# A linear-attention and mixture-of-experts kernel: other places for the routing and for the weight parts

## The chip, the cores and the metric

The kernel runs on one core of one Trainium2 chip. The core has five engines that each work through their own queue in order: TensorE (PE, with weight loads PEld), VectorE (DVE), ScalarE (ACT), GpSimd (POOL) and SyncE (SP, which here only issues DMAs). They wait for each other by semaphores. The metric is the device time of one execution in microseconds (us); of several runs the median counts.

## The reference

```python
def _attn_ref(r, k, v, w, u):                 # B, H, S, D = 4, 8, 768, 48
    state = zeros((B, H, D, D)); y = zeros_like(r)
    for t in range(S):
        kt, vt, rt = (k[:, :, t], v[:, :, t], r[:, :, t])
        cur = einsum('bhd,bhe->bhde', u[None] * kt, vt)
        y[:, :, t] = einsum('bhd,bhde->bhe', rt, state + cur)
        state = w[None, :, :, None] * state + einsum('bhd,bhe->bhde', kt, vt)
    return y

def _moe_ref(x, w_gate, w_noise, noise, w1, w2):   # N, D, E, F = 3072, 384, 8, 1024
    noisy_logits = x @ w_gate + log1p(exp(x @ w_noise)) * noise
    top2 = argpartition(-noisy_logits, 2, axis=1)[:, :2]
    top2_w = softmax of the two logits
    for e in range(E):
        for k in range(2):
            mask = top2[:, k] == e
            h = maximum(x[mask] @ w1[e], 0.0)
            out[mask] += top2_w[mask, k, None] * (h @ w2[e])
    return out
```
`reference()` runs the attention, lays its result out as 3072 tokens of 384 numbers, and gives that to the experts. All tensors are float32.

## The kernel before

**Attention.** The recurrence is cut into chunks of 128 steps: 6 chunks of 4 batches give NT = 24 tiles, in the order chunk by chunk. The loop over tiles (L958) is written so that neighbouring tiles overlap. One pass, here called turn i, puts out, in this order on each engine's queue:

- `load(i + 3)` on SP: k, r and v of a later tile.
- `trans(i + 1)`: TensorE transposes the decayed k (`kd`) and r; ScalarE copies the first to kT, VectorE multiplies the second into rT.
- `xtrans(i - 1)` and `zup(i - 1)`: the transposed output x of the tile before, and the state update (zt on VectorE, z and zb on ScalarE).
- `uterm_b(i + 1)`: a sum c on VectorE, then cv = v * c, on VectorE up to tile 8 and from tile 9 on as eight small ScalarE instructions (L327).
- `prep_k(i + 2)` and `uterm_a(i + 2)`: the products kd (L307) and rku (L314, L316) on GpSimd, each in two halves of 4 heads.
- one or two calls of `wstep` (weights, below), then `rstep(STEPS_A)` (routing, below).
- `yout(i)` on TensorE (L388 and L396), which needs the masked scores `am` of tile i; `xout(i)`: x on VectorE, and its store.
- `logits(i - 1)`, then `rstep(STEPS_B)`.
- `scores(i + 1)` on TensorE (L346; needs kT and rT), `mask(i + 1)` on VectorE (L354, two pieces), `kvup(i)` on TensorE (L364), then `rstep(STEPS_KV)`.

**Weights.** Each expert's W1 (three parts of 128 x 1024) and W2 (four parts of 128 x 768) is split into a high and a low part, so that products are nearly exact. A part is a generator in `w_split`: a DMA on SP into one of three staging buffers, then three empty places, then the copy of the high part on ScalarE (L279), then the subtraction of the low part on VectorE (L281). `wstep` moves each part in work on by one place and starts a new one if fewer than three are in work. Each call is one place.

**Routing.** The tiles fall into three groups of eight (GROUPS). When a group's logits are there, `route(g)` is queued: a generator of some 80 small VectorE instructions (noise term, the two largest logits, ranks, lists) with a few TensorE products among them. `rstep(us)` adds `us` to a credit, cuts the credit at 1.6 * us + 0.2, and then puts out routing until the credit is used up; most places of the generator cost 0.2. Where the generator says "pe", or where a group is newly queued, `at_pe` is set to `gap` = 2: the next call only counts down and returns, with its credit kept, and the one after it goes on. In turn 22 (I_EARLY) the lists of expert 0's first 512 tokens must be there, and its first tokens are gathered.

**Experts.** `seq` lists pieces (expert, chunk): expert 0 has three, the others two. A piece is `p1` (first product, eight steps of 9 products L841, then a ReLU on ScalarE L843 and a low part on VectorE L845) and `p2` (second product, L875, in groups of 128 tokens). `xT` transposes gathered tokens for the next piece. While expert 0's later pieces run, `rest(1)` and `rest(2)`, the lists of the other experts, are put out by `rest_step`; they use products with `pL` (L513) on TensorE. Expert 1's weights are queued ahead of `p2(0, 1)`, with three places at once, then two per group of tokens there and one per step of `p1(0, 2)`. From expert 1 on, one place per step carries the next expert's weights.

Of the kernel before, what the change touches and what calls it, by code (L numbers as in the profile page):

```python
# [25 lines left out]
W_MAX = 1.05  # L26
WARM0 = 8
STEPS_A = 1.2
STEPS_B = 1.1
STEPS_KV = 0.3  # L30
STEPS_P1 = 0.75
STEPS_P2 = 3.0
WARM1 = 2
# [9 lines left out]
def kernel(  # L43
# [14 lines left out]
    nc = tc.nc  # L58
    B, H, S, D = r.shape
# [198 lines left out]


    W = {}  # L260

    def w_split(e):
        W[e] = {}
        units = []

        def unit(mat, c0, c1, src):
            def f():
                if mat not in W[e]:
                    sh = [128, ND, FF] if mat == 0 else [128, NF, DM]
                    W[e][mat] = [wpool[e % 2].tile(sh, F32R, name=f"w{mat}{x}{e % 2}", bufs=1) for x in "hl"]  # L270
                hi, lo = (t[:, c0:c1, :] for t in W[e][mat])
                t = stg.tile([128, 1024], F32, name="stg")
                n = hi.shape[1] * hi.shape[2]
                tv = t[:, :n].rearrange("p (a b) -> p a b", b=hi.shape[2])
                nc.sync.dma_start(tv, src)
                yield
                yield
                yield
                nc.scalar.activation(hi, tv, AF.Copy)  # L279
                yield  # L280
                nc.vector.tensor_sub(lo, tv, hi.bitcast(F32))  # L281
                yield
            return f()

        for c in range(ND):
            units.append(unit(0, c, c + 1, w1[e, c * 128:(c + 1) * 128, :].rearrange("(c p) f -> p c f", p=128)))
        for c in range(0, NF, 2):
            units.append(unit(1, c, c + 2, w2[e, c * 128:(c + 2) * 128, :].rearrange("(c p) d -> p c d", p=128)))
        return units
# [3 lines left out]
    def wstep():  # L293
        for un in list(wrun):
            if next(un, 0) == 0:
                wrun.remove(un)
        if wq and len(wrun) < 3:
            un = wq.pop(0)
            next(un)
            wrun.append(un)  # L300
# [2 lines left out]
    AM, X, CV, PY, PA = {}, {}, {}, {}, {}  # L303

    def prep_k(i, eng=None):
        for h in (slice(0, H // 2), slice(H // 2, H)):
            (eng or nc.gpsimd).tensor_mul(kd[i % 3][:, h, :D], kt[i][:, h], tabk[:, h, :D])  # L307

    RKU = {}

    def uterm_a(i):
        rku = att.tile([128, H, D], F32, name="rku")
        for h in (slice(0, H // 2), slice(H // 2, H)):
            nc.gpsimd.tensor_mul(rku[:, h], rt[i][:, h], kt[i][:, h])  # L314
        for h in (slice(0, H // 2), slice(H // 2, H)):
            nc.gpsimd.tensor_mul(rku[:, h], rku[:, h], ub[:, h])  # L316
        RKU[i] = rku

    def uterm_b(i):
# [531 lines left out]
    def p2(e, ci, step=None):  # L851
        hb, ht = HH[e, ci]
        wh, wl = W[e][1]
        offs = {t: 128 * j for j, t in enumerate(chunks(e)[ci])}

        ts = chunks(e)[ci]
        for t in ts if (e, ci) != seq[-1] else ts[-1:] + ts[:-1]:
            n, o = tw(t), offs[t]
            py = psum.tile([128, DM], F32, name="pym", tag=f"py{np2[0] % 2}")
            np2[0] += 1  # L860
            ot = moe.tile([128, DM], F32, name="ot", bufs=NOT)
            OT[e, t] = ot
            hs = slice(o, o + n)
            if n == 64:
                for f in range(NF):
                    nc.tensor.matmul(py, ht[:, f].rearrange("p a b -> p (a b)"), wh[:, f, :], start=(f == 0), stop=(f == NF - 1),  # L866
                                     skip_group_check=True)
                    nc.tensor.matmul(py[:n], ht[:, f, 0, :], wl[:, f, :], start=False, stop=(f == NF - 1),  # L868
                                     skip_group_check=True)
                nc.scalar.activation(ot[:n], py[64:], AF.Copy)  # L870
                nc.vector.tensor_add(ot[:n], py[:n], ot[:n])
            else:
                q = [(a, x, f) for f in range(NF) for a, x in ((0, wh), (0, wl), (1, wh))]
                for j, (a, x, f) in enumerate(q):
                    nc.tensor.matmul(py, hb[:, f, a, hs], x[:, f, :], start=(j == 0), stop=(j == len(q) - 1))  # L875
                    if step and j % 8 == 7:
                        step()
                if (e, ci) == seq[-1]:
                    OT[e, t] = py
                else:  # L880
                    nc.scalar.activation(ot, py, AF.Copy)  # L881
            yield t
# [39 lines left out]

    gap, credit = [2], [0.0]

    def rstep(us):

        credit[0] = min(credit[0] + us, 1.6 * us + 0.2)
        while route_q:
            if at_pe[0] > 0:
                at_pe[0] -= 1  # L930
                if at_pe[0] > 0:
                    return
            if credit[0] <= 0:
                return
            try:
                c = next(route_q[0])
            except StopIteration:
                route_q.pop(0)
                continue
            if c == "pe":  # L940
                at_pe[0] = gap[0]
                credit[0] -= 0.3
                return
            credit[0] -= c or 0.2
# [13 lines left out]
    for i in range(NT):  # L958
        if i + NLD - 1 < NT and i + NLD - 1 > 2:
            load(i + NLD - 1)  # L960
        if i >= NT - 16:
            q = (i - NT + 16) * 192
            nc.sync.dma_start(out[q:q + 192, :].rearrange("(p two) d -> p two d", two=2),
                              zrow[:96, None, :].to_broadcast([96, 2, DM]))
        if i + 1 < NT:
            trans(i + 1)
        if i:
            xtrans(i - 1)
            zup(i - 1)
        if i == I_EARLY:  # L970
            while GEARLY - 1 not in routed:
                rstep(1)
            early()
        if i + 1 < NT:
            uterm_b(i + 1)
        if i + 2 < NT:
            prep_k(i + 2)
            uterm_a(i + 2)
        wstep()
        if i < GROUPS[0][1]:  # L980
            wstep()
        rstep(STEPS_A)
        if i == 0:
            flag = consts_c()
        if i in (0, 3):
            next(flag)
        yout(i)
        xout(i)
        if i:
            logits(i - 1)  # L990
            route_when_done(i - 1)
        rstep(STEPS_B)
        if i == NT - 1:
            for _ in xT(0, 0):
                pass
            p1a = p1(0, 0)
        if i + 1 < NT:
            scores(i + 1)
            mask(i + 1)
        kvup(i)  # L1000
        rstep(STEPS_KV)
    xtrans(NT - 1)
    next(p1a)
    logits(NT - 1)
# [28 lines left out]
    wts1 = stack.enter_context(tc.tile_pool(name="wts1", bufs=1, side="right", reuse_waits="tile"))  # L1033
    wpool[1] = wts1
    late[0] = stack.enter_context(tc.tile_pool(name="late", bufs=1, side="right", reuse_waits="tile"))
    wq.extend(w_split(1))
    for _ in range(3):
        wstep()
# [5 lines left out]
    def rest_step(us):  # L1044
        rstep(us)
        if not route_q and not listed[0]:
# [2 lines left out]
            xgather(1, 0)  # L1049
            tokens(NJ, E * NJ)  # L1050

    gap[0] = 1
    for t in p2(0, 1, lambda: rest_step(1.0)):
        if t == 3:
            for _ in xT(0, 2):
                pass
        hold.append((0, t))
        wstep()
        wstep()
    for s in range(2, len(seq)):  # L1060
        e, ci = seq[s]
        end = s + 1 == len(seq)
        if e and ci == 0:
            nxt = w_split(e + 1) if e + 1 < E else []
            wq.extend(nxt[:ND])
        elif e:
            wq.extend(nxt[ND:])
        xt = xT(*seq[s + 1]) if not end else iter(())
        for j, _ in enumerate(p1(e, ci)):
            while hold:  # L1070
                emit_out(*hold.pop(0))
            if s == 2:
                rest_step(STEPS_P1)
            elif XT_AT <= j < XT_AT + 2:
                next(xt, None)
            wstep()
        if s > 2 and s + 2 < len(seq):
            xgather(*seq[s + 2])

        for t in p2(e, ci, (lambda: rest_step(1.0)) if s == 2 else None):  # L1080
            if s > 2:
                next(xt, None)
            wstep()
            hold.append((e, t))
            while len(hold) > (0 if end else 1):
                emit_out(*hold.pop(0))
        if s == 2:
            while not listed[0]:
                rest_step(1)
            for _ in xt:  # L1090
                pass
            xgather(*seq[s + 2])
        if ci == len(chunks(e)) - 1 and not end:
            while hold:
                emit_out(*hold.pop(0))
            pgather(e + 1)
# [77 lines left out]
```

## Time and profile before

| | us |
|---|---|
| median of 3 runs (656.6 to 661.78) | 657.9 |
| the profiled execution | 665.16 |
| its span in the trace | 663.3 |
| attention, until its last scores | 170.29 |
| mean granted TensorE clock | 0.981 |

The profile shows one execution. A row of the view in order of time gives the start, the duration, the engine, the line, the operation with output and inputs, how many instructions are merged, and in brackets how long the engine had been idle before and what ended that. A row of the view by stretches gives the stretch, its length, then the busy time and the number of instructions of PE, PEld, DVE, ACT and POOL, the granted TensorE clock as a share of full speed, the DMA engines' mean busy share, and GB/s. On the page, each digit of "PEclk" is the granted clock in tenths in one of 40 equal slices. SPq is the time in which SP issues DMAs.

### The profile page before, as it was taken

Reading aid. Unit: us, or ns where it says so; the run is one execution under the profiler, and the core shown is the slowest. Engines: PE = TensorE matmul, PEld = TensorE weight load, DVE = VectorE, ACT = ScalarE, POOL = GpSimd, SP = SyncE. Lnnn points to the kernel's source line nnn. Section 1 sums busy time; section 2 is a strip of 40 time slices with the busy share of each in tenths; the row PEclk is TensorE's granted clock in tenths of the full one; section 3 lists DMA queues with packets and bytes.
Section 4 is the critical chain, followed back from the end, with each engine's and each line's share of the span. In section 5 each row is a group of like instructions: output and inputs, shape, how many; then the busy total and the mean of one; then the engine's idle time right before and its main releaser. Section 6 shows DMA issues by size and latency. Waiting matters only on the chain.

```text
span 663.3 us, 11905 instructions
## 1 busy us (share of the span) xinstructions
PE 631.3 (95%) x4436; PEld 600.9 (91%) x4437; DVE 352.1 (53%) x883; ACT 262.2 (40%) x737; POOL 260.6 (39%) x389
## 2 busy tenths in 40 slices
PE   8899899989998799999999999999999999999993
PEld 5789899988898789999999999999999999999993
DVE  7687868699479946253443625244262524523230
ACT  2455667666322424252442424234242433423220
POOL 8575534544201227422641542364164136315211
PEclk9889979999999999999999999999999999999998
DMA  7995746764304534441524334263343425302001
GB/s 127 221 238 130 168 113 169 160 152 117 109 1 128 161 126 134 132 142 70 186 82 139 117 113 136 69 186 100 121 127 108 130 78 175 103 26 85 37 2 37
DMA packets 111444, 78.87 MB, mean 119 GB/s; under 512 B 86721, under 2 KB 101441, under 8 KB 111378
## 3 DMA queue, kind: packets, MB, share of 16 engines
q1 hardware_dynamic: 101442, 49.19, 28.7%
q0 software_dynamic: 9936, 28.83, 13.9%
q8 instruction: 37, 0.61, 0.4%
q14 instruction: 29, 0.24, 0.1%
HBM read 59.03 MB, written 19.76 MB: 119 GB/s over the span
## 4 chain that ended last, share of the span: by engine, by line
PE 83%; DVE 9%; SPq 2%; issue 2%; ACT 2%; DMA 1%; POOL 0%; POOLq 0%; DVEq 0%; ACTq 0%
PE ph L841 31%; PE pym L875 30%; PE py L396 5%; PE pa L346 3%; PE ptm L820 3%; PE py L388 2%; PE pt L334 2%; PE pl L426 2%; SPq L122 2%; PE pym L868 2%; PE pym L866 2%; DVE am L354 1%; PE pwarm L364 1%; DMA stg<-in_moe_w_dram 1%; PE ptx L414 1%
## 5 line engine op out<-in xcount | busy, mean ns | idle before, releaser
L875 PE MATMUL pym<-w1h,hb 128*128 128x384 f32 x768 | 204.2, 339 | 0.0
L841 PE MATMUL ph<-xh,w0h 128*128 128x384 f32 (+3 forms) x408 | 142.6, 350 | 1.7 <-ACT xh L821 1.7
L896 POOL DMA_INDIRECT out_dram<-ot,TK x56 | 57.5, 1027 | 218.8 <-DVE ot L892 199.5
L841 PE MATMUL ph<-xl,w0h 128*128 128x384 f32 (+3 forms) x408 | 139.8, 343 | 0.5 <-DVE xl L822 0.2
L875 PEld LDWEIGHTS pym<-w1h,hb 128*128 128x128 f32 x768 | 139.6, 188 | 0.6
L841 PE MATMUL ph<-xh,w0l 128*128 128x384 f32 (+3 forms) x408 | 139.7, 342 | 0.0
L845 DVE SCALAR_TENSOR_TENSOR hb<-ph,hb 128x384 fp32r<-128x384 f32 (+1 forms) x136 | 72.5, 533 | 113.9 <-ACT ht L843 71.1
L875 PE MATMUL pym<-w1l,hb 128*128 128x384 f32 x384 | 129.5, 337 | 0.0
L843 ACT ACTIVATE hb<-ph 128x384 fp32r<-128x384 f32 (+1 forms) x136 | 64.2, 472 | 120.2 <-PE ph L841 112.7
L793 POOL DMA_INDIRECT xg<-xd,GR x56 | 53.7, 959 | 81.0 <-DVE f L675 34.2
L881 ACT ACTIVATE ot<-pym 128x384 f32<-128x384 f32 x45 | 22.1, 491 | 160.3 <-PE pym L875 160.3
L841 PEld LDWEIGHTS ph<-xh,w0h 128*128 128x128 f32 x408 | 77.3, 189 | 5.0 <-ACT xh L821 2.3
L841 PEld LDWEIGHTS ph<-xl,w0h 128*128 128x128 f32 x408 | 77.5, 190 | 3.7 <-DVE xl L822 1.2
L841 PEld LDWEIGHTS ph<-xh,w0l 128*128 128x128 f32 x408 | 77.3, 190 | 2.5
L875 PEld LDWEIGHTS pym<-w1l,hb 128*128 128x128 f32 x384 | 72.3, 188 | 0.1
L822 DVE TENSOR_TENSOR xl<-ptm,xh 128x384 fp32r<-128x384 f32 (+1 forms) x56 | 28.9, 524 | 75.1 <-ACT xh L821 53.0
L396 PE MATMUL py<-vt,am 128*128 128x96 f32 x384 | 61.3, 287 | 5.9 <-DVE am L354 5.3
L802 POOL DMA_INDIRECT pv<-out_dram,GA x49 | 55.6, 1135 | 25.9 <-issue 14.3
L396 PEld LDWEIGHTS py<-vt,am 128*128 128x128 f32 x384 | 52.9, 201 | 7.5 <-DVE am L354 7.5
L307 POOL TENSOR_TENSOR kd<-kt,tabk 128x192 f32<-128x192 f32 x46 | 27.2, 612 | 66.1 <-PE pwarm L364 58.1
L354 DVE TENSOR_TENSOR am<-pa,mneg 128x512 int32<-128x512 int32 x48 | 30.8, 682 | 12.4 <-PE pa L346 12.4
L892 DVE SCALAR_TENSOR_TENSOR ot<-ot,GT,pv 128x384 f32<-128x384 f32 (+1 forms) x46 | 27.0, 610 | 11.0 <-ACT ot L881 10.9
(206 smaller groups left out, 880.5 us busy)
## 6 DMA issues: line engine op xcount, KB each, us to landing
stg<-in_moe_w_dram SPq DMA_DIRECT2D x24, 512.0 KB, 4.1
stg<-in_moe_w_dram SPq DMA_DIRECT2D x32, 384.0 KB, 3.3
rd<-in_r_dram SPq DMA_DIRECT2D x24, 192.0 KB, 3.8
vt<-in_v_dram SPq DMA_DIRECT2D x24, 192.0 KB, 3.5
xd<-x SPq DMA_DIRECT2D x24, 192.0 KB, 2.0
out_dram<-zrow SPq DMA_DIRECT2D x16, 288.0 KB, 3.6
kt<-in_k_dram SPq DMA_DIRECT2D x23, 192.0 KB, 3.4
xg<-xd,GR POOLq DMA_INDIRECT x56
```

The costliest lines, as they stand in the source:

```text
L307: (eng or nc.gpsimd).tensor_mul(kd[i % 3][:, h, :D], kt[i][:, h], tabk[:, h, :D])
L354: nc.vector.tensor_tensor(am[:, s].bitcast(I32), pa[s].bitcast(I32), mneg.to_broadcast([128, NP, 128]), op=ALU.bitwise_and)
L396: nc.tensor.matmul(o2, AM[i][:, s, p, :], vt[i][:, h, None, :].to_broadcast([128, 2, D]), start=not c and h == 0, stop=h == H - 1, skip_gr ...
L793: nc.gpsimd.indirect_dma_start(out=xg[:n], out_offset=None, in_=xd[:GROUPS[GEARLY - 1][1] * 128] if early_ else xd, in_offset=bass.Indirec ...
L802: nc.gpsimd.indirect_dma_start(out=pv[:n], out_offset=None, in_=out, in_offset=bass.IndirectOffsetOnAxis(ap=GA[:n, e * NJ + t:e * NJ + t + ...
L822: nc.vector.tensor_sub(xl[:, :, o:o + n], pt[:, :, :n], xh[:, :, o:o + n].bitcast(F32))
L841: nc.tensor.matmul(ph[:, :w_], a[:, d, fs], x[:, d, :w_], start=(j == 0), stop=(j == len(q) - 1))
L843: nc.scalar.activation(h_[:, f, 0, :], ph[:, a:b], AF.Relu)
L845: nc.vector.scalar_tensor_tensor(h_[:, f, 1, :], ph[:, a:b], 0.0, h_[:, f, 0, :].bitcast(F32), op0=ALU.max, op1=ALU.subtract)
L875: nc.tensor.matmul(py, hb[:, f, a, hs], x[:, f, :], start=(j == 0), stop=(j == len(q) - 1))
L892: nc.vector.scalar_tensor_tensor(ot[:n], pt[:n], g, PV[e, t][:n], op0=ALU.mult, op1=ALU.add)
L896: st = nc.gpsimd.indirect_dma_start(out=out, out_offset=bass.IndirectOffsetOnAxis(ap=TK[:n, q:q + 1], axis=0), in_=ot[:n], in_offset=None, ...
```

## The change

Four things are changed together.

1. The three GpSimd products of a tile (and the one of tile 0 that VectorE does) are put out in one piece of 8 heads.
2. The call of `rstep` behind the mask adds no credit, and doesn't cut it either; the call ahead of the mask adds 1.2 where it added 1.1.
3. In the attention, weight parts have four empty places between load and copy where they had three; turns 0 and 1 have no place, turns 2 to 10 have two, later ones one. Before, turns 0 to 7 had two and later ones one.
4. Expert 1's first three places come with one empty place (NLAG = 1), and then its parts have no place until `p2(0, 2)`, where a place follows every eighth product and every group of tokens; in `p1(1, 0)` each step has two places.

```diff
-STEPS_B = 1.1
-STEPS_KV = 0.3
+STEPS_B = 1.2
...
+    NLAG = [4]
...
                 nc.sync.dma_start(tv, src)
-                yield
-                yield
-                yield
+                for _ in range(NLAG[0]):
+                    yield
                 nc.scalar.activation(hi, tv, AF.Copy)
                 yield
                 nc.vector.tensor_sub(lo, tv, hi.bitcast(F32))
...
     def prep_k(i, eng=None):
-        for h in (slice(0, H // 2), slice(H // 2, H)):
-            (eng or nc.gpsimd).tensor_mul(kd[i % 3][:, h, :D], kt[i][:, h], tabk[:, h, :D])
+        (eng or nc.gpsimd).tensor_mul(kd[i % 3][:, :, :D], kt[i], tabk[:, :, :D])
...
-        for h in (slice(0, H // 2), slice(H // 2, H)):
-            nc.gpsimd.tensor_mul(rku[:, h], rt[i][:, h], kt[i][:, h])
-        for h in (slice(0, H // 2), slice(H // 2, H)):
-            nc.gpsimd.tensor_mul(rku[:, h], rku[:, h], ub[:, h])
+        nc.gpsimd.tensor_mul(rku, rt[i], kt[i])
+        nc.gpsimd.tensor_mul(rku, rku, ub)
...
-    def rstep(us):
-
-        credit[0] = min(credit[0] + us, 1.6 * us + 0.2)
+    def rstep(us, cap=True):
+
+        if cap:
+            credit[0] = min(credit[0] + us, 1.6 * us + 0.2)
         while route_q:
...
-        wstep()
-        if i < GROUPS[0][1]:
+        for _ in range(0 if i < 2 else 2 if i < 11 else 1):
             wstep()
         rstep(STEPS_A)
...
         kvup(i)
-        rstep(STEPS_KV)
+        rstep(0, False)
...
+    NLAG[0] = 1
     wq.extend(w_split(1))
     for _ in range(3):
         wstep()
...
+    def mid():
+        rest_step(1.0)
+        wstep()
+
     gap[0] = 1
     for t in p2(0, 1, lambda: rest_step(1.0)):
...
         hold.append((0, t))
-        wstep()
-        wstep()
+    NLAG[0] = 3
     for s in range(2, len(seq)):
...
             elif XT_AT <= j < XT_AT + 2:
                 next(xt, None)
-            wstep()
+            if s > 2:
+                wstep()
+            if s == 3:
+                wstep()
...
-        for t in p2(e, ci, (lambda: rest_step(1.0)) if s == 2 else None):
+        for t in p2(e, ci, mid if s == 2 else None):
```

## The prediction

> **What bounds the kernel now.** I read the busy shares first, then the stretches, then TensorE in order of time, and last the queue of whatever its waits name.
>
> ```profile
> PE 631.3 (95%) x4436; PEld 600.9 (91%) x4437; DVE 352.1 (53%) x883; ACT 262.2 (40%) x737; POOL 260.6 (39%) x389
> ...
> PEclk9889979999999999999999999999999999999998
> ```
> ```profile
> 20.00:40.00 20.00, 15.90 (x168) 14.29 (x165) 15.04 (x23) 9.75 (x27) 14.06 (x21) 0.91 0.97 234
> ...
> 300.00:400.00 100.00, 100.00 (x569) 96.76 (x568) 39.65 (x75) 34.75 (x85) 43.03 (x53) 1.00 0.38 120
> ```
> TensorE bounds the kernel. In 300 to 400 us it never idles, and the change alters nothing there that a full TensorE would notice. What can be won or lost lies in its gaps before 250 us and in the slices whose granted clock is under 9. Call one pass of the attention loop (L958) a turn; the scores of the next tile (L346) mark it.
>
> ```profile
> 13.53 1.16 PE L346 MATMUL pa<-rT,kT 64*128 64x128 f32 x16
> ...
> 19.00 1.16 PE L346 MATMUL pa<-rT,kT 64*128 64x128 f32 x16
> ...
> 26.46 1.57 PE L426 MATMUL pl<-wg,xT 128*128 128x96 f32 x6 [2.69 <-ACT xT L416]
> ...
> 56.86 1.16 PE L346 MATMUL pa<-rT,kT 64*128 64x128 f32 x16
> ...
> 69.38 1.16 PE L346 MATMUL pa<-rT,kT 64*128 64x128 f32 x16
> ...
> 75.64 1.16 PE L346 MATMUL pa<-rT,kT 64*128 64x128 f32 x16
> ...
> 80.69 1.34 PE L396 MATMUL py<-vt,am 128*128 128x96 f32 x4 [1.85 <-DVE am L354]
> ...
> 87.08 2.08 PE L346 MATMUL pa<-rT,kT 64*128 64x128 f32 x16
> ...
> 95.27 1.16 PE L346 MATMUL pa<-rT,kT 64*128 64x128 f32 x16
> ```
> A clean turn lasts 19.00 - 13.53 = 5.47 us for the first four tiles and 75.64 - 69.38 = 6.26 us for the others. Turns 10 and 11 last 11.44 and 8.19: a wait for the mask, then half clock.
>
> ```profile
> 80.00:82.00 2.00, 1.18 (x5) 1.02 (x6) 1.97 (x7) 0.00 (x0) 0.55 (x2) 0.78 1.08 214
> ...
> 90.00:92.00 2.00, 2.00 (x13) 2.00 (x14) 1.47 (x7) 0.60 (x1) 2.00 (x5) 0.66 0.60 121
> ```
> The third last column is the granted clock: half speed from about 81.1 to 91.4. So a gap of 1.85 us was followed by about 10 us at half speed. TensorE's wait begins at 80.69 - 1.85 = 78.84, 3.2 after the scores; with the mask's two pieces (1.2 to 1.3 us, below) a mask that begins up to 2.0 after its scores costs nothing, and the next scores come 6.26 - 3.2 = 3.1 after TensorE goes on.
>
> **Step 1, weight loads leave the start: -8.0 us.**
>
> ```profile
> 18.35 1.18 SPq L275 DMA_DIRECT2D stg<-in_moe_w_dram  x2
> ...
> 24.41 1.06 ACT L279 ACTIVATE w0h<-stg 128x1024 fp32r<-128x1024 f32 x1 [5.70 <-DMA stg<-in_moe_w_dram]
> ```
> ScalarE waits 5.70 us for the first weight part; the transposed x (L416) is queued behind it, and TensorE waits 2.69 us for that. From turn 1 to turn 6 the loop takes 56.86 - 19.00 = 37.86 us, where clean turns need 2 x 5.47 + 3 x 6.26 = 29.72: 8.1 lost. In the new order the loads begin in turn 2, behind the loads of tile 5 on SP's queue, and ScalarE comes to a part four places, two turns, after its load. On SP two issues (1.18 us) now stand ahead of tile 6's loads, which have a turn to spare; per turn the DMAs carry a tile and at most two parts. I take 8.0 of the 8.1. The lower bound is 5: the DMA share is already 0.97 in this stretch, and the late part of the loss could return as a wait for k.
>
> **Step 2, the same parts run into the routing: +4.9, and 0.6 in step 3.** I count the places (two a turn from turn 2; a part has its ScalarE copy four places after its load and its VectorE subtraction one later; three in flight). The loads fall at places 1, 2, 3, 7, 8, 9 and 13. So the last W2 part has copy and subtraction at places 17 and 18, both in turn 10; the one before that at 13 and 14, both in turn 8. Before, the last subtraction was in turn 7. From turn 8 on, ScalarE also computes cv (L327), ahead of the part in its queue.
>
> ```profile
> 82.54 0.54 DVE L321 TENSOR_REDUCE c<-rku 128x8 f32<-128x384 f32 x1
> ...
> 84.44 1.91 ACT L327 ACTIVATE cv<-vt,c 128x48 f32<-128x48 f32 x8
> ...
> 56.11 0.84 ACT L279 ACTIVATE w1h<-stg 128x768 fp32r<-128x768 f32 x1
> ...
> 50.73 0.96 DVE L281 TENSOR_TENSOR w1l<-stg,w1h 128x768 fp32r<-128x768 f32 x1 [0.31 <-ACT w1h L279]
> ```
> By turn 10's own rows VectorE is free at 83.1 and would wait for a copy that ends at 86.3 + 0.84 = 87.2; its subtraction ends at 88.1. Behind it are queued the routing of this turn (1.9 us), x (0.5) and the mask, which then begins at 90.5. At full clock the scores begin at 80.7 + 3.1 = 83.8 and a mask at 85.8 is free: 4.7 late, 4.9 with waits on GpSimd.
>
> **Step 3, routing behind the mask grows instead of going: +3.1 in turns 8 to 10, +3.3 in turn 13, +3.0 in turns 16 to 18, +2.0 in turn 21.** The call behind the mask now adds no credit but also takes none away. While no routing is queued the credit fills to 1.6 x 1.2 + 0.2 = 2.12 (before, the last call cut it to 0.68). In turns 8 and 16 the call ahead of the mask only counts the TensorE gap down and returns; the call behind it then spends 2.12 at 0.2 a place: 14 instructions, where 6 stood.
>
> ```profile
> 70.57 1.29 DVE L354 TENSOR_TENSOR am<-pa,mneg 128x512 int32<-128x512 int32 x2 [1.20 <-PE pa L346]
> 71.78 0.40 DVE L555 SCALAR_TENSOR_TENSOR r_a<-lg 128x64 f32<-128x64 f32 x1
> 72.10 0.63 DVE L556 SCALAR_TENSOR_TENSOR r_zp<-lg,nz 128x64 f32<-128x64 f32 x1
> ...
> 74.40 0.68 DVE L339 TENSOR_TENSOR rT<-pt,pwr 128x512 f32<-128x512 f32 x1
> ...
> 76.45 0.74 DVE L453 SCALAR_TENSOR_TENSOR r1q<-r1q,r1r 128x64 f32<-128x64 f32 x3
> 77.11 0.55 DVE L404 TENSOR_TENSOR x<-py,cv 128x384 f32<-128x384 f32 x1
> ...
> 80.01 1.22 DVE L354 TENSOR_TENSOR am<-pa,mneg 128x512 int32<-128x512 int32 x2
> ...
> 183.16 0.22 DVE L555 SCALAR_TENSOR_TENSOR r_a<-lg 128x64 f32<-128x64 f32 x1
> ```
> ```profile
> 70.94 1.15 POOL L307 TENSOR_TENSOR kd<-kt,tabk 128x192 f32<-128x192 f32 x2 [2.91 <-PE pwarm L364]
> 72.05 1.14 POOL L314 TENSOR_TENSOR rku<-rd,kt 128x192 f32<-128x192 f32 x2
> ```
> The 8 extra instructions (four of them like L453's, 0.25 each; some 1.75 us) push rT from 74.40 to 76.15; it ends at 76.75, and the scores due at 75.64 wait 1.1 us. By the next mask 27 routing instructions have passed instead of 18: 76.75 + 0.7 (state update and c) + 13 x 0.25 + 0.5 (x) = 81.2, and 2.0 of waiting for GpSimd's next products (step 4), so it begins near 83.2 instead of 80.01. Its scores begin at 76.75: 83.2 - 76.75 - 2.0 = 4.45 late. The two waits are 5.5 against 80.01 - 75.64 - 2.0 = 2.4 now: +3.1, and 0.6 for the part subtracted in turn 8. In turn 11 the call ahead of the mask again only counts down; 11 instructions stand behind it, so that rT ends 6.1 after that turn's scores; then c (6.9), 9 more (8.3), x (8.8) and 4, three of which wait for a product (11.5). The next mask is 11.5 - 6.26 - 2.0 = 3.3 late where it costs nothing now.
>
> ```profile
> 134.94 1.16 PE L346 MATMUL pa<-rT,kT 64*128 64x128 f32 x16
> ...
> 143.67 1.16 PE L346 MATMUL pa<-rT,kT 64*128 64x128 f32 x16
> ```
> The second group of tiles repeats turn 8 in turn 16, without weights: its turn of 8.73 holds 2.5 of waiting now; the same count gives 5.5, +3.0. In turn 19, 8 instructions behind the mask delay rT and the mask after it: +2.0 by the same count, the least certain. A slightly shorter turn 15 gives 0.4 back.
>
> **Step 4, products in one piece.** Under a product the 0.22 us instruction takes 0.40, its follower 0.63: one VectorE instruction passes per half product of 0.57.
>
> ```profile
> 1.55 0.56 POOL L155 MEMSET kd<- 128x128 f32 x3
> ...
> 2.83 1.50 POOL L231 MEMSET zb<- 128x384 f32 x4
> ```
> A fill of 384 takes 0.375, one of 128 0.19, so some 0.1 of each is fixed and is saved where two halves are joined. I put a whole product at 1.0 (two halves less 0.1; 0.85 to 1.15 for the range). Off routing, GpSimd has slack and the gain is nothing. Under routing, one VectorE instruction per 1.0 us would pass instead of one per 0.57; this is inside step 3 (some 2.8 us of its sum).
> These rows don't show what a longer product does. [...]
>
> **Step 5, expert 1's parts: -1.5 us.**
>
> ```profile
> 213.41 1.22 DVE L281 TENSOR_TENSOR w0l<-stg,w0h 128x1024 fp32r<-128x1024 f32 x1
> ...
> 219.05 2.35 DVE L281 TENSOR_TENSOR w0l<-stg,w0h 128x1024 fp32r<-128x1024 f32 x2
> ```
> ```profile
> 210.66 0.49 ACT L881 ACTIVATE ot<-pym 128x384 f32<-128x384 f32 x1 [4.95 <-PE pym L875]
> ```
> ```profile
> 213.55 0.51 PE L513 MATMUL pL<-r_ob,r_oa 128*128 128x98 bf16 x8 [1.54 <-DVE r_ob L509]
> ...
> 230.42 0.52 PE L513 MATMUL pL<-r_ob,r_oa 128*128 128x98 bf16 x8 [2.56 <-DVE r_ob L509]
> ```
> The first copies, one place behind their loads, wait for the DMA in the 4.95 us in which ScalarE has nothing else. The first subtraction moves ahead of the list work: the gap of 1.54 grows by 1.2. The other two (2.35) and the W2 parts leave the first product, where VectorE makes TensorE wait 2.56 and lose half of 3.4 us at half clock: -4.3. In expert 0's last product the last part's copy (0.84) stands ahead of expert 1's x on ScalarE: +0.85. The two places a step in expert 1's first product cost nothing: VectorE and ScalarE are under half busy in such a stretch (300 to 400 us). Sum -2.2; I take -1.5, since a gap of 2.7 may itself lower the clock (+1.7).
>
> **Step 6, the clock: +1.3.** Half clock costs turns 10 and 11 now 4.7 (11.44 - 6.26 - 2.4 and 8.19 - 6.26). The new waits of 3.5 to 5 us each bring at least one stretch of 3.4 us at half speed, 1.7 lost, hidden where another mask is late anyway: three full ones and half of a fourth, 6.0.
> [...]
>
> **Sum:** -8.0 + 4.9 + 0.6 + 3.1 + 3.3 + 3.0 + 2.0 - 0.4 - 1.5 + 1.3 = +8.3 us. The profiled execution takes 665.16 (span 663.3); it becomes 673.5. It lies 1.1% above the median of the runs, 657.9, which becomes 666.2; I say 666. Ends: -2 (waits 13 for 16.5, no half clock, step 5 at -2.2) to +18 (the start's 5, waits 19, half clock 9, step 5 at +0.2).
>
> **Rivals.**
> - *The late weight parts hold nobody up.* If turn 10's copy gets ahead of cv, or its subtraction falls into time in which TensorE is at half clock anyway, the 5.5 of step 2 goes, and with it a stretch of half clock: 666 - 7 = 659, no change. For it: TensorE is slow there now. It decides when the mask of turn 10 starts within 1.9 us of its scores. Against it: the order of ScalarE's rows in step 2.
> - *The routing moves ahead of the mask as the change's words say*, nothing being left to spend behind it: the 11.0 of step 3 goes: 655. Against it: the call behind the mask was seen spending in turn 8, and nothing in the new one empties the credit.
> - *The start doesn't get faster*, its 8 us being DMA time: 671 to 674. For it the share of 0.97, against it that about 1 MB leaves that stretch.
> - *Both first ones hold*, and the start's gain is left: 648.
>
> **How the numbers follow.** Within 1% of 657.9 (651.3 to 664.5) is about what a measurement of this kernel can't tell from no change. Chances: the forecast 0.45 (own range 660 to 674: slower 0.34, same 0.11), late parts that hold nobody up 0.15 (same 0.13, the rest 0.01 each side), routing as the words say 0.12 (same 0.09, faster 0.03), no faster start 0.17 (slower), both 0.11 (faster). Slower 0.52, same 0.33, faster 0.15. The range 652 to 676 leaves out about a tenth at each end.
>
> **What would show it.** Right: turns 1 to 6 take about 30 us; VectorE has 14 routing instructions between the mask and rT in turn 8; a W2 subtraction in turn 10 waits for ScalarE; masks of turns 9, 10, 12 and 17 begin over 5 us behind their scores; VectorE's small instructions under a product take about 1 us; no gap near 230 us. Wrong: those masks begin within 4 us, or the product's pieces don't hold VectorE longer.

## The result, and the profile after

The changed kernel takes 680.53 us in the median of four runs (678.96 to 682.2), the kernel before 657.25 (656.54 to 661.78): ratio 1.032, 95% interval 1.027 to 1.038 (the ratios here are recorded estimates with their intervals; the plain quotient of these two medians is 1.035). The profiled execution takes 681.34 (span 679.6). The forecast was 666, with a range up to 676: the side was right, the size was not. Medians and means in this document leave out executions that lie over 1.5% above the fastest of their kernel: one of ten of places_only (671.06), one of four of credit_only (3469.91, at full clock, its cause unknown), four of ten of early_lag3 (667.38 to 670.25). The page of the kernel after, granted clock in 40 slices:

```profile
PEclk9999786989799897999999999999999999999997
```
Apart from the last slice, three were under 9 before, all ahead of 100 us; now there are seven, five of them between 68 and 187 us. In order of time, some of TensorE's scores (L342; L346 before) and of its waits over 1 us look like this:

```profile
19.45 1.16 PE L342 MATMUL pa<-rT,kT 64*128 64x128 f32 x16
...
49.26 1.16 PE L342 MATMUL pa<-rT,kT 64*128 64x128 f32 x16
...
61.78 1.16 PE L342 MATMUL pa<-rT,kT 64*128 64x128 f32 x16
65.86 0.55 PE L410 MATMUL ptx<-ident,x 128*128 128x128 f32 x3 [1.41 <-DVE x L400]
71.76 1.16 PE L342 MATMUL pa<-rT,kT 64*128 64x128 f32 x16
77.79 1.34 PE L392 MATMUL py<-vt,am 128*128 128x96 f32 x4 [2.83 <-DVE am L350]
84.18 2.08 PE L342 MATMUL pa<-rT,kT 64*128 64x128 f32 x16
...
105.23 1.34 PE L392 MATMUL py<-vt,am 128*128 128x96 f32 x4 [3.12 <-DVE am L350]
...
184.11 1.16 PE L342 MATMUL pa<-rT,kT 64*128 64x128 f32 x16
```
Turns 2 to 6 take 49.26 - 19.45 = 29.81 us, 8.05 less than before. From there to the last scores the loop takes 134.85 us where it took 113.43: 21.4 more, all of it behind turn 8. What these 21.4 are is read from the view by stretches, from the scores of turn 8 to the last ones (after, then before):

```profile
61.80:184.10 122.30, 107.59 (x1033) 101.22 (x1032) 90.57 (x268) 66.10 (x234) 41.56 (x41) 0.85 0.51 123
```
```profile
69.40:170.30 100.90, 95.11 (x1035) 89.87 (x1034) 82.61 (x265) 64.67 (x231) 46.28 (x80) 0.95 0.60 143
```
TensorE's work is the same (1033 and 1035 records), but it is busy for 107.59 us instead of 95.11, because its granted clock is 0.85 instead of 0.95. So 12.5 of the 21.4 us are slower TensorE, and 8.9 are idleness (14.7 instead of 5.8). The view of waits names the idleness:

```profile
PE py L392 <- DVE am L350: 8.1, 4, 3.1
PE ptx L410 <- DVE x L400: 5.0, 3, 1.8
PE pa L342 <- DVE rT L335: 1.2, 1, 1.2
```
(In all, how often, the longest.) Before, the mask cost 4.8 in three waits, x and rT nothing in this part. After the attention the two profiles differ by 2.5 us, and TensorE is busy for 476.30 us there instead of 473.76: that is slower clock, too (granted 0.96 instead of 0.99 until 300 us).

The stretches of half clock lie on a grid. Cut at its edges, two of them read:

```profile
74.88:78.29 3.41, 0.55 (x3) 0.30 (x2) 3.31 (x7) 0.50 (x2) 1.58 (x2) 1.00 1.03 215
78.29:81.71 3.42, 3.32 (x16) 3.32 (x16) 1.37 (x4) 2.42 (x9) 0.00 (x0) 0.50 0.17 57
81.71:85.12 3.41, 3.41 (x20) 3.24 (x21) 1.39 (x7) 2.14 (x8) 0.00 (x0) 0.50 0.00 0
85.12:88.53 3.41, 3.41 (x35) 3.10 (x32) 3.00 (x22) 0.37 (x1) 1.36 (x2) 0.50 0.34 85
88.53:91.95 3.42, 3.42 (x33) 3.42 (x32) 2.89 (x17) 2.75 (x10) 1.60 (x2) 1.00 0.99 224
102.19:105.60 3.41, 0.37 (x2) 0.30 (x2) 3.41 (x4) 1.06 (x4) 1.75 (x2) 1.00 0.69 153
105.60:109.01 3.41, 3.27 (x16) 3.19 (x16) 2.02 (x5) 2.29 (x9) 0.00 (x0) 0.50 0.67 167
```
After a stretch in which TensorE worked 0.55 of 3.41 us it has half clock for exactly three stretches, 10.2 us; then full clock. The same follows the wait for the mask of turn 13.

### The profile page after: what moved, and what is told of

Read it like the earlier page. It is cut to its first block, busy times and chain, and to the rows that moved or that the text cites. A ratio compares the mean times of both kernels' runs of the same rounds, so it can differ in the third digit from the quotient of the medians.

```text
span 679.6 us, 11833 instructions
## 1 busy us (share of the span) xinstructions
PE 642.5 (95%) x4436; PEld 612.4 (90%) x4437; DVE 359.5 (53%) x882; ACT 262.5 (39%) x737; POOL 249.4 (37%) x318
## 4 chain that ended last, share of the span: by engine, by line
PE 66%; DVE 3%; ACT 1%; issue 0%; POOL 0%; POOLq 0%
PE ph L837 31%; PE pym L871 29%; PE ptm L816 2%; PE pym L864 2%; PE pym L862 2%; DVE xl L818 0%; DVE r_oa L496 0%; DVE hb L841 0%; PE pL L509 0%; ACT xh L817 0%; PE py L392 0%; DVE ot L890 0%; PE pl L422 0%; DVE w0l L280 0%; DVE r_ob L503 0%
## 5 line engine op out<-in xcount | busy, mean ns | idle before, releaser
L392 PE MATMUL py<-vt,am 128*128 128x96 f32 x384 | 66.6, 304 | 8.8 <-DVE am L350 8.1
L392 PEld LDWEIGHTS py<-vt,am 128*128 128x128 f32 x384 | 57.7, 216 | 10.8 <-DVE am L350 10.5
L305 POOL TENSOR_TENSOR kd<-kt,tabk 128x384 f32<-128x384 f32 x23 | 23.2, 1007 | 85.3 <-PE pwarm L360 75.0
L280 DVE TENSOR_TENSOR w1l<-stg,w1h 128x768 fp32r<-128x768 f32 x32 | 31.7, 993 | 11.9 <-ACT w1h L278 11.9
```

Of the source, the lines that this page charges most:

```text
L305: (eng or nc.gpsimd).tensor_mul(kd[i % 3][:, :, :D], kt[i], tabk[:, :, :D])
L392: nc.tensor.matmul(o2, AM[i][:, s, p, :], vt[i][:, h, None, :].to_broadcast([128, 2, D]), start=not c and h == 0, stop=h == H - 1, skip_gr ...
```

## The experiments

Each run also records its span and mean granted clock. Span x (1 - clock) is what half clock took from it: cut at the edges of the grid, the profiles show a granted clock of 0.50 or 0.51, or of 0.99 or 1.00. For the kernel before (19 runs beside the first four kernels) the spans scatter by 2.7 us (standard deviation), but span less this loss by 1.0: its run-to-run spread is mostly the clock. Means over runs, us; the ratio is against the kernel before on the same chip, while the medians of one table row and another can come from different chips. Only the change itself is over 2% slower with its whole interval; for smaller differences the interval says how far they are clear of chance.

| kernel | median | ratio, 95% | mean span | half clock | the rest |
|---|---|---|---|---|---|
| before | 660.18 | | 658.8 | 9.4 | 649.4 |
| after | 680.53 | 1.032 (1.027 to 1.038) | 678.8 | 26.0 | 652.8 |
| places_only | 665.15 | 1.005 (1.002 to 1.009) | 662.8 | 12.6 | 650.2 |
| credit_only | 674.2 | 1.016 (1.008 to 1.025) | 671.1 | 15.9 | 655.2 |
| whole_only | 670.06 | 1.012 (1.004 to 1.020) | 668.1 | 15.0 | 653.1 |
| expert1_only | 660.14 | 0.999 (0.995 to 1.002) | 658.5 | 8.0 | 650.5 |
| all_filled | 674.45 | 1.019 (1.011 to 1.028) | 673.1 | 9.6 | 663.5 |
| all_empty | 668.4 | 1.011 (1.003 to 1.020) | 667.5 | 14.2 | 653.3 |
| all_halves | 675.8 | 1.020 (1.011 to 1.029) | 673.9 | 18.2 | 655.7 |
| early_lag3 | 661.67 | 0.999 (0.994 to 1.005) | 659.1 | 9.6 | 649.6 |
| before_filled | 659.37 | 0.996 (0.993 to 1.000) | 657.2 | 7.9 | 649.3 |
| expert1_lag3 | 663.35 | 1.004 (1.001 to 1.008) | 661.4 | 10.9 | 650.5 |
| early_expert1 | 661.65 | 1.002 (0.999 to 1.005) | 659.8 | 12.5 | 647.2 |
| early_expert1_filled | 658.46 | 0.998 (0.995 to 1.001) | 657.1 | 8.0 | 649.1 |
| early_filled | 654.11 | 0.992 (0.989 to 0.995) | 653.0 | 5.8 | 647.1 |
| early_part4_filled | 655.71 | 0.994 (0.992 to 0.997) | 654.1 | 6.7 | 647.4 |

From before to after the mean span grows by 20.0 us: 16.6 of them are half clock, 3.4 the rest.

### Each part alone

**places_only** (part 3; NLAG is 4 for expert 0 and 3 from expert 1 on):
```diff
-                yield
-                yield
-                yield
+                for _ in range(NLAG[0]):
+                    yield
...
-        wstep()
-        if i < GROUPS[0][1]:
+        for _ in range(0 if i < 2 else 2 if i < 11 else 1):
             wstep()
```


> Before with part 3 alone (four empty places; no place in turns 0 and 1, two in turns 2 to 10). Theory (the routing carried behind the mask, and the longer products, make masks late, and each late mask brings half clock; the weights' move gains at the start and pays in turns 8 to 10): turns 1 to 6 about 8 us shorter, turns 8 to 11 together 5 to 9 us longer, turns 12 to 21 as before; in all 652 to 660. Rival (the weight parts of turns 8 and 10 are the main cost of the change): 668 or more.

It took 665.15, between the two forecasts. Turns 2 to 6 took 29.9 us in its profile, 8.0 less than before, and turns 8 to 11 together 37.53, 5.4 more than the 32.15 before, as the theory had it. This is the share of the last W2 part (VectorE, then TensorE):

```profile
80.72 1.30 DVE L281 TENSOR_TENSOR w1l<-stg,w1h 128x768 fp32r<-128x768 f32 x1 [4.05 <-ACT w1h L279]
```
```profile
84.94 0.90 PE L414 MATMUL ptx<-ident,x 128*128 128x128 f32 x3 [4.32 <-DVE x L404]
```
The subtraction waits 4.05 us for a copy that stands behind cv; x is queued behind it, and TensorE waits 4.32 us. But turns 17 to 21, which this part of the change doesn't touch and the theory had as before, took 4.6 us more. Their wait for the mask has the same row in both profiles; here it stands between the grid of the kernel before and that of places_only:

```profile
135.79:139.20 3.41, 2.36 (x35) 2.01 (x33) 3.20 (x9) 3.38 (x13) 2.69 (x5) 1.00 0.33 85
139.20:142.61 3.41, 2.47 (x20) 2.31 (x21) 3.34 (x11) 0.74 (x4) 0.66 (x2) 1.00 0.78 161
142.61:146.02 3.41, 3.41 (x50) 3.14 (x49) 3.24 (x17) 3.15 (x14) 0.78 (x2) 1.00 0.44 137
```
```profile
138.02 1.34 PE L396 MATMUL py<-vt,am 128*128 128x96 f32 x4 [1.86 <-DVE am L354]
```
```profile
134.84:138.25 3.41, 1.55 (x15) 1.39 (x13) 3.27 (x8) 2.49 (x10) 3.04 (x6) 1.00 0.49 117
138.25:141.66 3.41, 3.32 (x16) 3.11 (x16) 3.20 (x13) 1.63 (x6) 0.00 (x0) 0.51 0.84 205
141.66:145.07 3.41, 3.41 (x20) 3.24 (x21) 1.49 (x11) 2.20 (x10) 0.00 (x0) 0.50 0.10 34
```
Before, the edge of a stretch cuts the 1.86 us in two (busy 2.36 and 2.47 of 3.41), and the clock stays. In places_only it falls into one stretch (busy 1.55), and three stretches at half clock follow (138.25 to 148.48 us). In these two profiles one wait of one length costs nothing or some 5 us, by where the grid lies.

**credit_only** (part 2):
```diff
-STEPS_B = 1.1
+STEPS_B = 1.2
...
+        if cap:
+            credit[0] = min(credit[0] + us, 1.6 * us + 0.2)
...
-        rstep(STEPS_KV)
+        rstep(0, False)
```


> Before with part 2 alone (no credit added or cut behind the mask, 1.2 ahead of it). Theory: late masks in turns 9, 12 or 13, 17 and 20 or 21, without the longer lock of the whole products: +8 of waiting and 3 to 7 of half clock, 667 to 673. Rival (the whole products are the main cost, the credit costs little without them): under 662.

674.2, ratio 1.016, 1 us above the theory's range: part 2 alone is half of the whole loss. In its profile turns 9, 13, 18 and 21 are longer than before by 1.2, 4.6, 4.1 and 2.4 us, the places that the theory named. What the theory calls the longer lock is only seen as time: under half products of 0.57 us the instructions of L556, L441 and L455 take 0.63, 0.52 and 0.52 us in before; under whole ones of 1.00 us the same three (L553, L438, L452) take 1.03, 0.91 and 1.04 in whole_only. No row shows what holds them.

**whole_only** (part 1):
```diff
-        for h in (slice(0, H // 2), slice(H // 2, H)):
-            (eng or nc.gpsimd).tensor_mul(kd[i % 3][:, h, :D], kt[i][:, h], tabk[:, h, :D])
+        (eng or nc.gpsimd).tensor_mul(kd[i % 3][:, :, :D], kt[i], tabk[:, :, :D])
... (rku likewise)
```


> Before with part 1 alone (products in one piece). Theory: only the routing that stands between the mask and rT and ahead of the next mask passes more slowly: +3 to +6, 660 to 664. Rival (the whole products are the main cost): 668 or more. A second rival (a longer product holds VectorE no longer than two halves): within 2 us of before.

670.06, ratio 1.012 (+2.8 to +13 us): dearer than the forecast for this run and within the rival's range, though the rival's words (the main cost) don't hold: credit_only costs no less. Of the 9.3 us by which its mean span is longer, 5.6 are half clock and 3.7 the rest. Its waits for the mask:

```profile
80.43 1.34 PE L393 MATMUL py<-vt,am 128*128 128x96 f32 x4 [3.07 <-DVE am L351]
...
141.19 1.30 PE L393 MATMUL py<-vt,am 128*128 128x96 f32 x4 [3.08 <-DVE am L351]
```
Each is 1.2 us longer than before (1.85 and 1.86). The second brought 6.8 us of half clock in this profile, where the shorter one before brought none.

**expert1_only** (part 4; the rest as in the change's diff from NLAG = 1 on):
```diff
+    NLAG[0] = 1
     wq.extend(w_split(1))
...
-        wstep()
-        wstep()
+    NLAG[0] = 3
```

> Before with part 4 alone (expert 1's parts moved out of the first product of expert 0's last piece). Forecast: -1.5, between -4.3 and +3, that is 653 to 661; the gap near 213 us grows by about 1.2, that near 230 us goes. Rival (the longer gap brings a stretch of half clock worth more than it saves): 659 to 662.

660.14 against 660.18: no difference. Part 4 is not where the time went. The four ratios add up to +0.5 + 1.6 + 1.2 - 0.1 = 3.2%, and the change cost 3.2%: the parts need no effect on one another to explain the whole, though each interval is near a per cent wide.

### Parts taken back, and the clock by itself

**all_empty**: the changed kernel, with the credit emptied behind the mask.
```diff
         kvup(i)
+        credit[0] = min(credit[0], 0.0)
         rstep(0, False)
```


> The changed kernel, but the credit is set to at most 0 ahead of the call behind the mask, so that it puts out no routing at all, as the change's words have it. Theory (routing carried behind the mask makes masks late): the waits of turns 9, 10 and 13 shrink to under 1.5 us, in all 662 to 671. Rival (weight parts and longer products are the main cost, wherever the routing stands): 676 or more.

668.4, 12 less than the change, within the theory's range, although not all of its waits went: the last W2 part now has its 4.19 us, and turn 22, in which TensorE waits 5.53 us for the routing left over (L506), lasts 13.8 us instead of 6.1.

**all_halves**: the changed kernel with part 1 taken back.
```diff
-        (eng or nc.gpsimd).tensor_mul(kd[i % 3][:, :, :D], kt[i], tabk[:, :, :D])
+        for h in (slice(0, H // 2), slice(H // 2, H)):
+            (eng or nc.gpsimd).tensor_mul(kd[i % 3][:, h, :D], kt[i][:, h], tabk[:, h, :D])
... (rku likewise)
```

> The changed kernel with the products in halves again. Part 1 alone cost 1.2% on the kernel before. If parts 1 and 2 add up: 672 to 674. If the longer lock costs more where more routing stands behind the mask: 664 to 670. If it is already hidden behind the other waits: 677 or more.

675.8, 4.7 less than the change by the medians, which come from different chips. By the ratios it is about 1.2% less (some 8 us), as much as part 1 cost alone. The first number lies between the first and the third case, the second would mean that the parts add up; the intervals (ratios 1.011 to 1.029 here, 1.027 to 1.038 for the change) don't decide.

**all_filled**: the changed kernel with products of zeros, their result unused, in the gaps.
```diff
+    def fill(n, tag):
+        if n:
+            pf = psum.tile([128, 512], F32, name="pf", tag=tag)
+            for _ in range(n):
+                nc.tensor.matmul(pf, wsrc[:, :128], wsrc, start=True, stop=True)
...
+        fill({9: 4, 18: 5, 21: 5}.get(i, 0), "py1")
         if i:
             xtrans(i - 1)
...
+        fill({10: 8, 13: 8, 18: 4, 21: 2}.get(i, 0), "py0")
         yout(i)
```


> The changed kernel with 36 products of zeros (bf16, 128 x 512, some 0.4 us each, 14 us of added TensorE work, results unused) put into the gaps of TensorE: ahead of the transposed x in turns 9, 18 and 21 (4, 5, 5) and ahead of the masked product in turns 10, 13, 18 and 21 (8, 8, 4, 2). Theory (the gaps lower the granted clock, and half clock is the larger part of what the change costs): the stretches at 78.8 to 88.4, 105.8 to 116, 146.7 to 153.5 and 170.5 to 177.4 us go or shrink, mean clock 0.975 to 0.985, in all 664 to 674, though TensorE has more to do. Rival (VectorE's queue sets the pace there, half clock only fills time in which TensorE would wait): 678 to 690.

674.45: 6.1 less, with 36 more products to do (put at 0.4 us each; five in a row took 1.24 us in before_filled, 0.25 each); half a us above the theory's range, below the rival's. Half clock took 9.6 us instead of 26.0, and of 37.5 us of it between 65 and 180 us in the profile 10.2 were left (89.7 to 99.9). The rest grew by 10.7, the fillers and the waits that half clock had covered. So half clock is a cost of its own, but part of it hid waits.

### What the start's gain comes to

**early_lag3**: before, with the places of part 3, but the copy three places after the load as before (four in part 3); the last part is split in turn 9.
```diff
-        wstep()
-        if i < GROUPS[0][1]:
+        for _ in range(0 if i < 2 else 2):
             wstep()
```


> Before with the weight parts' places of part 3 (none in turns 0 and 1, two a turn from turn 2) but three empty places as before, so that the last part is split in turn 9. Theory (the start gains, and only parts split in turn 8 and later, behind cv on ScalarE and beside the routing, cost): turns 2 to 4 last 5.4 to 6.5 us, turn 10 is no longer than before, in all 648 to 656. Rival (two places a turn cost VectorE and ScalarE as much later as the start gains): 658 to 664.

661.67, ratio 0.999: no difference, and in the rival's range, though its profiled execution ended the attention at 161.71 us instead of 170.29. Turn 10 has one wait more than before (there the mask's 1.85 us stood alone), so the early places do cost something later:

```profile
72.59 0.55 PE L414 MATMUL ptx<-ident,x 128*128 128x128 f32 x3 [1.18 <-DVE x L404]
...
75.16 1.06 PE L396 MATMUL py<-vt,am 128*128 128x96 f32 x4 [1.82 <-DVE am L354]
```
Without half clock that turn lasts 8.71 us with the old places (before_filled, below) and 10.11 with the early ones (early_filled). After the attention this execution took 6.8 us more than before: 3.2 of them are TensorE at a lower clock, 3.3 a wait for a stall of ScalarE (last section).

**before_filled**: before, with `fill` of all_filled ahead of `yout` in two turns.
```diff
+        fill({10: 5, 18: 5}.get(i, 0), "py0")
         yout(i)
```

> The kernel before with ten products of zeros (5 ahead of the masked product in turn 10, 5 in turn 18), where it waits 1.85 and 1.86 us for the mask. Theory (half clock follows a gap of about 1.3 to 1.9 us or more in one stretch of 3.41 us, and costs up to 5 us around turn 10): no half clock between 75 and 95 us, turns 10 and 11 last 8 to 9 and 6.3 instead of 11.44 and 8.19, 653 to 657. Rival (half clock there only fills time in which VectorE's queue sets the pace): 658 to 662.

659.37, in the rival's range: by the ratio a small gain (0.996, up to 1.000), by the medians (659.53 for the kernel before on that chip) none. Turns 10 and 11 took 8.71 and 6.26 us at full clock in its profile, as the theory had it; so the mechanism came and the gain in time did not.

**expert1_lag3**: part 4 without the lines that set NLAG, so that a part always has three empty places.
```diff
+    def mid():
+        rest_step(1.0)
+        wstep()
...
         hold.append((0, t))
-        wstep()
-        wstep()
```

> Part 4 alone, but its first parts keep three empty places, so that no subtraction stands ahead of the list work. Theory (part 4 traded a gap of 2.56 us for one of 2.72): the gap near 213 us stays at 1.5, the one near 230 us shrinks to about 0.8, no half clock between 200 and 250 us, 655 to 659. Rival (those gaps cost nothing that shows): 659 to 661.

663.35, slower than forecast. The gaps went as the theory said (1.54 and 0.82), but a new wait came ahead of expert 1's first product: 4.88 us for the token's low part (L822), behind expert 1's W2 subtractions on VectorE, whose copies wait for their loads. The forecast had not asked what is late next.

**early_expert1** (the diffs of early_lag3 and expert1_lag3 together) and **early_expert1_filled** (with that of before_filled, too):

> The early places of early_lag3 and the moved parts of expert1_lag3 together. Theory (each takes gaps away, and neither lengthens a late mask): attention ends near 162 to 166 us, no half clock between 200 and 250 us, 652 to 659. Rival (the gaps' stretches of half clock only fall elsewhere): 660 to 664.

> The kernel of early_expert1 with the ten products of before_filled. Theory: its time less 3 to 6, 648 to 655, mean clock 0.99 or more. Rival (the filling takes TensorE as much time as the clock gives): no less than early_expert1.

661.65 and 658.46: the first in the rival's range, the second slower than the theory's range, but 3.2 less than the first, as forecast. The wait of expert1_lag3 is in both (4.75 and 4.70 us).

**early_filled**: early_lag3 with fillers, and **early_part4_filled**, the same with part 4 as in the change.
```diff
+        fill({10: 3}.get(i, 0), "py1")
         if i:
             xtrans(i - 1)
...
+        fill({10: 5, 18: 5}.get(i, 0), "py0")
         yout(i)
```

> early_lag3 with 13 products of zeros: 3 ahead of the transposed x and 5 ahead of the masked product in turn 10, 5 ahead of the masked product in turn 18. Theory (the start's gain of about 5 us is real, and early_lag3 gave it back as half clock around turns 10 and 18 and in the list work): mean clock 0.987 or more, 652 to 657. Rival (the gain is lost to other waits, or isn't there): 658 to 662.

> The kernel of early_filled with part 4 of the change as it is. Part 4 alone made no difference (ratio 0.9986), and gave the highest mean clock of the kernels tried so far (0.988). Theory: its time is that of early_filled less 0 to 3, 650 to 657. Rival (the longer first gap of the list work brings half clock here): 1 to 3 more than early_filled.

654.11, ratio 0.992 (0.989 to 0.995): faster than both kernels, and within the theory's range. Part 4 adds nothing to it (655.71, in the rival's range). The page of early_filled:

```profile
PEclk9999999999999999999999999999999999999998
```
So with fillers most of the start's gain is there: early_filled's mean span is 5.2 us under the 658.2 of the kernel before on that chip. That early_lag3 lost it to the clock alone isn't shown. Against early_lag3, early_filled has 3.8 us less half clock and 2.5 less of the rest; but early_lag3 has only 1.0 more half clock than the kernel before on its own chip (9.6 and 8.6). Part of the gain may be the fillers' own, as before_filled's interval overlaps that of early_filled.

## Why the prediction was off

- **Step 6, the clock, is the step that failed.** It put +1.3 us: 6.0 for the new waits, about one stretch each, less the 4.7 that was there. Measured from turn 9 on, TensorE's work took 12.5 us longer: eleven stretches of half clock (37.5 us) instead of three. Its rows held the sign against it (one gap of 1.85 us, then three stretches), but it priced each new wait at half of one stretch, 1.7 us, as the shortest ones in the profile of before have it (3.42 us each at 26.56 and 231.36 us, at 0.51 of full clock). The longest waits (2.83 and 3.12) brought three stretches each, the others one or two. The runs bear it out: of 20.0 us more in the mean span 16.6 are half clock, and all_filled, with more for TensorE to do, had 16.4 us less of it and was 6.1 faster.
- **The whole sum.** Between the profiled executions the change costs 16.2 us, where the sum had 8.3: 11.2 more from the clock, 7.6 less from the waits, 4.0 more after the attention, and 0.4 in the first turns. The medians differ by 23.3; the other 7 are the baseline, as the profiled execution of before lay 7.9 us over its median and that of after only 0.8.
- **Steps 2 and 3 were right in place and too large in size.** They put 16.5 us of waits behind turn 8; 8.9 came as idleness. The masks of turns 9, 12 and 17 begin 5.3, 5.6 and 6.0 us behind their scores, as forecast, that of turn 10 only 2.7. In turn 8, 14 routing instructions stand between the mask and rT, as counted (66.93 to 69.77 us; the row of L449 holds four):

```profile
65.73 1.27 DVE L350 TENSOR_TENSOR am<-pa,mneg 128x512 int32<-128x512 int32 x2
66.93 0.43 DVE L551 SCALAR_TENSOR_TENSOR r_a<-lg 128x64 f32<-128x64 f32 x1
...
68.85 1.00 DVE L449 SCALAR_TENSOR_TENSOR r1q<-r1q,r1r 128x64 f32<-128x64 f32 x4
69.77 0.68 DVE L335 TENSOR_TENSOR rT<-pt,pwr 128x512 f32<-128x512 f32 x1
...
73.65 3.23 DVE L573 SCALAR_TENSOR_TENSOR r_q<-r_q,r_s 128x64 f32<-128x64 f32 x4
...
83.69 0.96 DVE L280 TENSOR_TENSOR w1l<-stg,w1h 128x768 fp32r<-128x768 f32 x1 [4.04 <-ACT w1h L278]
```
  The part subtracted in turn 8, put at 0.6, made TensorE wait 1.41 us for x. The last row is step 2's late part in turn 10, behind cv as said. In the changed kernel TensorE doesn't wait for it: it runs at half clock from 78.3 to 88.5. The first rival named just this ("falls into time in which TensorE is at half clock anyway"), but took a stretch of half clock off for it, where half clock had to be there to hide it. In places_only and all_empty, where TensorE came there at full clock, the same part cost 4.3 and 4.2 us.
- **Step 4's rate was right; its cost by the clock was left out.** One whole product takes 1.00 us (forecast 1.0), and four small VectorE instructions took 3.23 us under three of them:

```profile
73.51 1.00 POOL L305 TENSOR_TENSOR kd<-kt,tabk 128x384 f32<-128x384 f32 x1 [6.23 <-PE pwarm L360]
74.47 1.00 POOL L311 TENSOR_TENSOR rku<-rd,kt 128x384 f32<-128x384 f32 x1
75.55 0.99 POOL L312 TENSOR_TENSOR rku<-rku,ub 128x384 f32<-128x384 f32 x1
```
  That is about one VectorE instruction per product. Why it takes that long isn't shown; the rows of before have half products alone, so for a whole one it was the author's estimate. The 2.8 us was counted within step 3, for new routing alone, and no run shows this term by itself. In its place whole_only shows that the longer product also meets the routing that stood there before: 7.9 us by the ratio, and in the mean span 3.7 of waits and work and 5.6 of half clock.
- **Step 1** came out at 8.05 us between the two profiles, but 8 is not what an execution usually loses there. The profiled execution of before lay 8 us over its median, and had two stretches of half clock in turns 2 to 6 (26.5 to 29.9 and 40.2 to 43.6 us). In four other profiles with the old start and halves (credit_only, expert1_only, before_filled, expert1_lag3) these turns take 33.3, 35.6, 36.5 and 34.3 us, not 37.9: against 30 the gain is nearer 5. So the agreement of 8.05 with 8.0 owes much to the one execution that both were read from: the sum took a loss of that execution for a loss of the kernel, and then moved the result to the median.
- **Step 5** put -1.5; expert1_only measured no difference (-3.5 to +1.6, which holds -1.5 as well). As it had said, the first gap grew and the second went (1.54 to 2.72 and 2.56 to 0.82):

```profile
228.33 0.69 PE L509 MATMUL pL<-r_ob,r_oa 128*128 128x98 bf16 x8 [2.72 <-DVE r_ob L505]
...
244.92 0.52 PE L509 MATMUL pL<-r_ob,r_oa 128*128 128x98 bf16 x8 [0.82 <-DVE r_ob L505]
```
- **The rivals.** "The routing moves ahead as the words say" was wrong, as argued: all_empty had to add a line for it, and took 12 us less (step 3 had put 11.0). "The start doesn't get faster" was wrong.

## What to carry to other kernels

Price a new wait of TensorE by what it leaves of the clock afterwards, not by its length: here idleness of 2 us within 3.4 cost up to 5 us more (1.86 us in places_only, then three stretches at half clock). Set a sum against what an execution usually loses in a stage; one profiled execution may hold losses of its own, and its mean clock beside that of other runs tells so. Where a wait can't be removed, a few unused products in it can be worth trying: 13 of them with a change of weight places that alone gave nothing made 0.8%; ten of them without it made 0.4%, or perhaps nothing.

## What the runs showed of the hardware

- **A grid of 3.413 us.** In 15 profiles every edge of half clock (16 to 290 us) lies on one grid of 3.413 us per execution, within 0.2 us; its phase differs from one execution to the next (modulo 3.413: 2.7 before, 3.2 after, 1.7 in places_only, 0.5 in expert1_only). A phase that differs would explain why one kernel's runs differ; the runs without a trace can't show it.
- **How much idleness lowers the clock.** Counted per stretch of that grid: of the full-clock stretches with 1.89 us of idleness or more, all 33 were followed by half clock; with less than 1.22, none; between the two, 17 were and 29 weren't. Half clock lasted one stretch (26 times), two (12), three (11) or four (1). What decides between one and three stretches wasn't found.
- **A stall of ScalarE with no cause that the profile names.** In early_lag3:

```profile
263.87 0.49 ACT L843 ACTIVATE hb<-ph 128x384 fp32r<-128x384 f32 x1 [3.84 <-remote]
```
  The profile names no tile and no engine for it. It held TensorE up there:

```profile
264.42 0.69 PE L875 MATMUL pym<-w1h,hb 128*128 128x384 f32 x1 [3.30 <-ACT hb L843]
```
  Such stalls of 1.6 to 7.3 us stand in eight of the first ten profiles, between 608 and 624 us or between 165 and 285; TensorE waits for none of the others (before: 2.57 us ahead of 610.75, with TensorE busy all the time). What ScalarE waits for stays open.
